# A new order for the first half of a hand-ordered kernel: w_in split ahead of w_out, one triangular mask scaled on ScalarE

## The chip, the cores and the metric

The kernel runs on one core of a Trainium2 chip. The metric is the device time of one execution in microseconds (us). Engines are named as the profile names them: PE (TensorE, matrix multiply), PEld (its weight loads), DVE (VectorE), ACT (ScalarE), POOL (GpSimd), SP (SyncE, which here only issues DMAs).

## What is computed

Three layers follow each other. The first is a linear attention with a per-channel decay, for 2 batches, 8 heads, 768 positions and 48 channels a head:

```python
for t in range(S):
    kt, vt, rt = (k[:, :, t], v[:, :, t], r[:, :, t])
    cur = np.einsum('bhd,bhe->bhde', u[None] * kt, vt)
    y[:, :, t] = np.einsum('bhd,bhde->bhe', rt, state + cur)
    state = w[None, :, :, None] * state + np.einsum('bhd,bhe->bhde', kt, vt)
```

The second, on rows of 384, is a gated convolution: `h = max(x @ w_in, 0)` (384 to 1024), a convolution of three taps along the sequence, a sigmoid of it as the gate, and `(h * gate) @ w_out` (1024 to 384). The third is a mixture of 8 experts (384 to 1024 to 384) in which every row goes to one expert; a row may keep the expert of the row before it.

## The kernel before

Attention is done in 12 chunks of 128 positions (`i` = 0 to 11, six a batch), the gated convolution in 3 groups of about 256 positions a batch and 4 pairs of 128 hidden columns (24 gates `G_b_g_fp`), its second product in 12 tiles of 128 rows, and the experts after that, on rows that are scattered to slots in DRAM and gathered back.

Each piece of work is a Python generator, and each `yield` ends a step. The string `SEQ` (lines 51 to 105) is a list of tokens; one token runs one generator by one step (`advance`, L1161). PE, ACT, DVE and SP execute what the steps emit strictly in that order, each on its own queue, so the order of the tokens is the order of every queue; POOL keeps program order too (`pool_order`, L1167). There is no planner: an instruction whose operand is late holds up everything behind it on its engine.

The tokens that matter here:

- `C` (constants, L253): step 12 makes the identities `id16` (DVE) and `idk` (ACT). Step 13 makes two masks from the triangle `tri0`, both on DVE: `tri32` (L289), which masks the scores of chunks 1 to 5, and `tri` (L290), for chunks 6 to 11. Chunk 0 uses `tri0` itself.
- `L_i` (L188): three loads k, r, v of chunk i. `A_i` (`decay`, L331): POOL scales r and k, PE transposes them (`ptf`), ACT (or DVE) copies them out as `rT`, `kT`; POOL multiplies the two to `kr`.
- `Y_i` (`scores`, L458): PE `psa` (scores), two masked copies `am` on DVE, PE `psy`, for chunks with a state PE adds `psy` from `z`, DVE `yt`, PE transposes (`pxf`), ACT writes the high half of `x1T`, DVE the low half (L511). `Z_i`: the state (PE `psu`, DVE `z`, ACT copies of z). `B_i`: PE `psd`, DVE `dv`.
- `WI_q` (`load_w_in`, L537): a quarter of `w_in`. SP loads it, DVE narrows it from 64 to 32 bits in three instructions (`narrow`, L177, on `f`), ACT scales it and makes the high half (L528, L529), POOL the low half `wi_l` (L156). Quarter q holds the columns of pair fp = q.
- `WO_q` (`load_w_out`, L580): a quarter of `w_out`, two row tiles; each is narrowed on DVE into PSUM (on `ps`), ACT makes the high half, DVE the low half; later PE transposes it and multiplies it with the gate weights.
- `G_b_g_fp` (`gate`, L620): PE `psh` (9 matmuls that read `x1T` and `wi_h`, `wi_l`), ACT `hp`, the three taps (on PE, or ACT and DVE), ACT tanh, DVE `cv`, ACT `g_h`, POOL `g_l`. `H_k` (L241): two matmuls on zeros that nobody reads.
- `O`, `OL`, `OR` (L678): the second product; `R`, `Q`, `S` (route, chances, scatter); `RC`, `SI`: constants of the routing and the clearing of the slots; `W1`, `W2`: expert weights, each loaded by SP, split by ACT (L533) and DVE (L158).

All loads of `w_in`, `w_out`, `W1` and `W2` take turns in three staging buffers (tag `stage`, `bufs=3`): the fourth load waits until the first one's tile has been narrowed or split, and the SP queue waits with it.

Of the kernel before, what the change touches and what calls it, by code (L numbers as in the profile page):

```python
# [55 lines left out]
A_4 CV G_0_0_0 G_0_0_1 A_4 WO_1 Z_3 WO_0 WO_1 Y_3 G_0_0_1 Z_3 L_5 WO_0 L_6 WO_2 Y_3 L_5 G_0_0_1 L_7 Y_2 Z_2 WO_1 A_4 Y_2 A_5 G_0_0_1 A_4 WO_0 WI_2 Y_2  # L56
G_0_0_1 A_4 WO_0 Y_3 Y_2 WO_0 L_6 G_0_0_1 A_5 WO_0 G_0_0_1 Y_4 WO_2 Y_3 A_5 WO_0 B_3 A_5 WI_2 Y_3 WI_2 Z_4 A_5 WO_1 B_3 Z_3 WO_2 L_6 WO_1 Y_4 L_6 WO_2
G_0_0_0 WO_1 G_0_0_2 Z_4 L_7 A_6 T WO_1 A_5 G_0_0_1 WO_1 G_0_0_0 G_0_0_2 A_6 WO_2 B_6 A_5 G_0_0_0 WO_2 B_4 A_6 G_0_0_1 G_0_0_2 Y_3 B_4 WO_2 G_0_0_0
G_0_0_2 Y_3 Y_4 G_0_0_0 Y_3 W1_5_0 A_6 G_0_0_2 Y_5 Y_3 Y_4 G_0_0_0 B_6 Z_4 G_0_0_2 Y_5 G_0_0_2 A_6 WO_1 G_0_0_2 G_0_1_1 A_6 B_6 WO_1 SI G_0_0_2 WO_2
G_0_1_1 G_0_0_2 WO_1 Y_4 A_6 B_5 WO_1 A_6 Y_4 Z_6 L_7 WO_2 A_6 G_0_0_0 WO_1 RC B_5 Y_5 G_0_0_2 G_0_1_2 G_0_1_1 L_7 A_7 G_0_0_0 G_0_1_1 G_0_1_2 G_0_1_1  # L60
G_0_1_2 Y_4 G_0_0_2 Z_6 G_0_1_2 B_7 G_0_1_1 G_0_1_1 WO_3 G_0_1_2 G_0_1_0 G_0_1_2 WO_2 Y_5 G_0_1_2 WO_2 Y_4 A_6 L_10 G_0_1_1 Y_5 Y_6 L_8 G_0_1_2 L_8
G_0_1_1 G_0_1_2 L_8 L_8 G_0_1_1 A_7 G_0_1_2 WO_3 G_0_1_0 G_0_1_0 Y_6 WO_2 Y_6 G_0_1_0 G_0_1_1 WO_3 A_7 G_0_1_0 A_7 A_8 Y_5 A_7 G_0_1_1 G_0_0_3 Z_6 A_7
G_0_0_3 WO_2 L_9 WO_3 WO_3 A_7 Y_5 WO_2 G_0_1_0 G_0_1_0 G_0_1_0 A_7 L_10 B_6 A_8 WO_3 L_9 G_0_1_3 G_0_1_0 WO_2 A_8 Y_6 WO_3 Y_5 G_0_0_3 B_7 WO_2 WO_2
Z_6 A_7 Z_7 G_0_1_3 A_8 L_9 G_0_0_3 G_0_0_3 G_0_1_3 G_0_1_3 G_0_1_3 G_0_0_3 G_0_1_2 G_0_0_3 G_0_1_2 G_0_1_0 O_0_0 Y_5 A_8 G_0_1_3 G_0_0_3 Y_4 G_0_1_3
O_0_0 A_7 G_0_1_3 WO_3 A_8 B_7 G_0_0_3 WO_3 Y_7 G_0_0_3 Y_7 O_0_0 WO_3 G_0_2_0 A_8 B_8 A_8 G_0_1_3 Y_6 L_9 WO_3 WO_3 G_0_1_3 WO_3 WO_3 L_11 B_8 Z_7
A_9 G_0_2_1 B_7 Y_6 Y_7 G_0_0_3 WO_3 G_0_0_3 Y_7 G_0_2_0 WO_3 G_0_1_3 A_9 Z_8 G_0_2_0 G_0_2_1 WO_3 A_8 Z_8 B_8 G_0_1_3 Y_8 Z_7 G_0_2_0 G_0_2_0 Y_6
G_0_2_0 A_9 L_10 G_0_2_1 G_0_2_0 G_0_2_0 Y_6 Y_7 G_0_2_1 G_0_2_1 G_0_2_1 B_9 O_0_1 A_9 Y_7 G_0_2_1 G_0_2_0 Z_7 G_0_2_0 L_10 G_0_2_0 G_0_2_2 A_9 A_9
G_0_2_2 Y_7 G_0_2_1 G_0_2_0 Y_8 O_0_2 A_9 O_0_2 O_0_1 B_9 Y_8 RC G_0_2_1 G_0_2_1 G_0_2_1 Z_8 O_0_2 O_0_0 B_8 G_0_2_3 A_10 O_0_2 Z_9 A_9 O_0_2 A_9 Y_7
G_0_2_1 Y_8 O_0_0 Y_9 Y_8 G_0_2_2 O_0_1 O_0_0 Y_9 Y_8 L_11 G_0_2_3 G_0_2_2 L_11 A_10 G_0_2_2 Y_7 Y_8 O_0_1 O_0_0 O_0_3 G_0_2_2 A_10 A_10 L_11 Y_8
O_0_1 G_0_2_2 G_0_2_2 O_0_1 Y_8 Z_8 G_0_2_3 O_0_1 Y_9 A_10 G_0_2_3 A_10 G_0_2_3 O_0_3 O_0_4 G_0_2_2 A_10 G_0_2_2 O_0_2 A_10 G_0_2_3 O_0_4 G_0_2_3  # L70
G_1_0_3 G_1_0_3 O_0_2 G_0_2_3 Y_9 A_10 G_1_0_3 A_11 Y_10 G_0_2_2 G_0_2_2 A_11 G_1_0_3 Y_9 A_11 B_9 G_1_0_3 G_0_2_3 G_1_0_3 B_10 G_1_0_3 G_0_2_3 W1_6_0
A_11 O_0_3 G_1_0_3 G_0_2_3 G_1_0_3 G_1_0_1 G_0_2_3 O_0_4 G_1_0_3 A_11 O_0_3 Y_10 G_1_0_1 G_1_0_1 G_1_0_1 G_1_0_1 G_1_0_1 A_11 O_0_4 G_1_0_1 Y_10
G_1_0_1 B_9 G_1_0_3 G_1_0_1 O_0_5 O_0_5 Y_9 O_0_4 O_0_4 G_1_0_1 A_11 O_0_5 O_0_3 G_1_0_3 B_10 O_0_4 O_0_5 B_10 G_1_0_0 G_1_0_2 Y_9 G_1_0_2 O_0_5 WO_0
Z_9 A_11 A_11 R_0_0_6 Z_9 O_0_3 Y_11 Y_9 Z_10 WO_1 O_0_3 Y_10 O_0_5 O_0_5 G_1_0_2 Z_10 B_11 G_1_0_0 G_1_0_1 Z_9 R_0_0_6 B_11 Y_11 Y_10 Z_10 R_0_0_6
B_10 R_0_0_6 Y_9 G_1_0_0 Y_10 G_1_0_0 Y_10 G_1_0_2 G_1_0_0 G_1_0_1 G_1_0_2 G_1_0_2 Z_10 B_11 Y_11 G_1_0_0 R_0_0_6 G_1_0_2 G_1_0_0 G_1_0_2 Y_10 R_0_0_6
R_0_0_6 Y_10 R_0_0_6 G_1_0_2 Y_11 G_1_0_0 R_0_0_6 B_11 G_1_0_0 Y_11 G_1_0_0 Y_11 Y_11 Y_11 Y_11 G_1_1_1 G_1_1_1 X G_1_1_1 G_1_0_2 G_1_1_1 R_0_0_6
G_1_1_1 G_1_0_2 G_1_1_2 OR_1_1 OL_1_0 G_1_1_1 G_1_0_2 OL_1_1 G_1_1_1 OL_1_1 G_1_1_2 W1_6_0 R_0_0_6 OL_1_1 G_1_1_1 R_0_0_6 OL_1_0 OL_1_1 OL_1_0 R_0_0_6
OL_1_1 W1_3_0 G_1_1_2 G_1_1_3 OL_1_0 G_1_1_1 G_1_1_2 OL_1_0 G_1_1_1 W1_5_0 R_1_0_2 G_1_1_3 G_1_1_2 SI G_1_1_3 Q_0_0_6 G_1_1_3 G_1_1_3 R_0_0_6 OR_1_1
G_1_1_1 R_0_0_6 G_1_1_3 G_1_1_3 G_1_1_2 OR_1_1 G_1_1_0 G_1_1_2 G_1_1_1 G_1_1_3 G_1_1_2 R_1_0_2 Q_0_0_6 G_1_1_3 G_1_1_3 W1_6_0 G_1_1_2 G_1_1_2 G_1_1_0
G_1_1_3 Q_1_0_2 W1_3_0 G_1_1_2 G_1_2_1 G_1_2_1 OR_1_1 G_1_1_3 Q_0_0_6 G_1_2_1 OR_1_1 G_1_1_0 S_5 G_1_2_1 G_1_1_0 G_1_1_0 G_1_2_1 G_1_2_1 G_1_1_0  # L80
G_1_1_0 G_1_2_1 W1_3_0 G_1_1_0 OR_1_0 OR_1_0 W1_0_0 R_1_0_2 G_1_1_2 G_1_2_3 OR_1_1 W1_0_0 G_1_2_1 S_4 OR_1_0 G_1_1_0 W1_5_0 G_1_2_3 G_1_2_3 G_1_2_3
G_1_2_3 OR_1_0 G_1_2_3 G_1_1_0 G_1_2_1 W1_7_0 Q_1_0_2 OL_1_2 S_2 S_1 R_1_0_2 G_1_2_1 OL_1_2 G_1_2_0 G_1_2_3 W1_7_0 OL_1_2 OL_1_2 OL_1_3 G_1_2_3 OL_1_2
OL_1_3 OL_1_3 G_1_2_0 G_1_2_3 G_1_2_1 OL_1_3 W1_7_0 G_1_2_0 OL_1_3 G_1_2_3 OR_1_0 R_1_0_2 R_1_0_2 G_1_2_0 G_1_2_1 G_1_2_0 G_1_2_3 G_1_2_2 G_1_2_2
R_1_0_2 IO R_1_2_2 G_1_2_2 R_1_0_2 W1_0_0 R_1_2_2 G_1_2_0 G_1_2_3 W1_1_0 S_0 G_1_2_0 R_1_0_2 G_1_2_2 OR_1_2 R_1_2_2 W1_4_0 S_3 Q_1_0_2 G_1_2_2 G_1_2_2
R_1_2_2 OR_1_2 W1_2_0 S_7 R_1_2_2 OR_1_0 Q_1_2_2 OL_1_0 G_1_2_0 G_1_2_2 G_1_2_0 OR_1_2 OR_1_3 WO_3 R_1_2_2 Q_1_2_2 G_1_2_0 OR_1_2 G_1_2_2 R_1_2_2 S_6
G_1_2_2 OR_1_3 FE R_1_2_2 Q_1_2_2 OR_1_2 G_1_2_2 OR_1_3 G_1_2_2 OR_1_3 OR_1_3 OR_1_2 W1_4_0 OL_1_5 R_1_2_2 OL_1_4 OL_1_4 S_8 OL_1_5 FE W1_2_0 OR_1_3
G_1_2_2 OL_1_4 OL_1_4 S_8 OL_1_4 OL_1_5 OL_1_5 OR_1_4 OR_1_4 OL_1_5 OL_1_1 R_1_4_2 W1_4_0 R_1_4_2 FE OR_1_5 S_9 VE R_1_4_2 R_1_4_2 W1_2_0 I_1 OR_1_4
R_1_4_2 ER OR_1_5 OR_1_4 I_3 I_0 ER W2_2_0 R_1_4_2 OR_1_5 R_1_4_2 R_1_4_2 Q_1_4_2 R_1_4_2 OR_1_5 W1_1_0 OH OH F OR_1_4 OR_1_4 Q_1_4_2 OR_1_5 EX EX
Q_1_4_2 OR_1_5 EX I_1 I_0 F EX W2_6_0 EX EX EX I_2 I_3 S_11 VE EX W1_1_0 EX S_10 EX EX EX F M W2_2_0 I_2 U_0_5 U_0_0 W2_2_0 U_0_1 EJ V I_10 V I_12
OL_1_2 U_0_1 U_0_0 S_7 S_6 W2_3_0 U_0_1 U_0_3 W2_6_0 U_0_2 U_0_3 W2_1_0 I_11 U_0_0 U_0_1 U_0_2 W2_3_0 I_10 U_0_4 U_0_3 U_0_4 U_0_0 U_0_2 I_6 U_0_2  # L90
U_0_4 U_0_5 I_11 U_0_1 I_13 S_10 U_0_3 U_0_10 U_0_11 W2_3_0 I_7 U_0_5 I_13 I_6 W2_7_0 U_0_0 U_0_3 I_7 W2_1_0 W2_1_0 I_8 U_0_13 W2_6_0 U_0_6 I_12 U_0_5
U_0_13 U_0_11 I_8 W2_7_0 I_9 U_0_13 OL_1_3 U_0_7 U_0_11 W2_5_0 U_0_13 WO_2 U_0_2 W2_4_0 I_9 W2_7_0 U_0_6 W2_0_0 U_0_11 U_0_10 U_0_10 U_0_12 U_0_10
D_0_5 W2_5_0 U_0_12 U_0_10 U_0_4 U_0_8 W2_5_0 S_11 W1_5_1 S_4 U_0_12 W2_4_0 ME U_0_8 U_0_13 U_0_12 W2_0_0 U_0_9 ME U_0_11 W2_4_0 W2_0_0 W1_6_1 U_0_12
D_0_4 D_0_0 W1_5_1 NX W1_7_1 D_0_13 D_0_5 W1_5_1 U_0_9 D_0_4 U_0_7 D_0_2 D_0_11 W1_6_1 D_0_2 W1_4_1 D_0_12 D_0_0 U_0_7 D_0_13 ME U_0_8 U_0_9 D_0_10
W1_6_1 D_0_3 U_0_7 D_0_11 U_0_8 W1_0_1 W1_4_1 W1_7_1 W1_4_1 D_0_1 U_1_4 W1_0_1 D_0_3 W1_3_1 S_5 W1_7_1 U_0_6 W1_0_1 S_1 U_1_5 W1_3_1 D_0_10 W1_2_1
# [1147 lines left out]
```

## Time and profile before

| | us |
|---|---|
| median of 3 runs (339.04 to 342.38) | 339.89 |
| the profiled execution | 340.96 |
| its span, first to last instruction | 339.2 |

The profile is of one execution. Its first page gives the busy time of each engine over the span and then, in 40 slices, how busy each was. Further views used here: busy times and the clock granted to PE in stretches (windows), the instructions of one engine in order of time (timeline), and the chain of waits that ended last. The start of the span is time zero everywhere below.

### The profile page before, as it was taken

The page shows a single profiled execution, that of the slowest core. Times are in us where ns is not written, and L with a number is a line of the kernel's source. Part 1 is how long each engine was busy: PE and PEld are TensorE (multiplying, and loading weights), DVE is VectorE, ACT ScalarE, POOL GpSimd, SP SyncE. Part 2 cuts the span into 40 slices and gives each one's busy share as a digit, 9 for nine tenths or more (in the row PEclk, how much of TensorE's full clock was granted, in tenths as well). Part 3 has the DMA queues.
Part 4 walks back from the last instruction along what each step waited for, and adds up shares of the span by engine and source line. Part 5 has one row for each costly group of instructions (what it writes and reads, how often), then busy time and mean ns, then how long its engine had stood idle before and what let it go on. Part 6 is the DMA issues. An engine that isn't in the chain of part 4 may idle for free.

```text
span 339.2 us, 8616 instructions
## 1 busy us (share of the span) xinstructions
PE 309.6 (91%) x3227; PEld 214.2 (63%) x3227; DVE 251.9 (74%) x494; ACT 193.0 (57%) x351; POOL 153.6 (45%) x206
## 2 busy tenths in 40 slices
PE   2977999999999999999789886999999998999992
...
GB/s 113 264 231 173 232 161 142 87 211 159 133 65 100 173 64 25 26 225 115 122 230 164 77 263 231 353 146 268 283 281 243 218 273 233 280 68 125 103 75 70
DMA packets 100707, 57.71 MB, mean 170 GB/s; under 512 B 80841, under 2 KB 90376, under 8 KB 100660
## 3 DMA queue, kind: packets, MB, share of 16 engines
...
q8 instruction: 29, 0.48, 0.6%
q14 instruction: 18, 0.15, 0.1%
...
## 4 chain that ended last, share of the span: by engine, by line
PE 44%; issue 33%; DVE 10%; POOL 5%; DMA 3%; ACT 2%; POOLq 1%; SPq 0%; ACTq 0%; DVEq 0%
PE psh L639 13%; PE psx L686 11%; PE pst L653 3%; PE psy L486 3%; PE psa L476 3%; POOL out_dram L905 3%; PE ps L653 2%; DMA slots<-xr,posi 2%; PE psy L498 2%; DVE w1l L158 1%; POOL yb L1017 1%; DMA raw<-in_r_dram 1%; PE psu L430 1%; DVE f L182 1%; PE ptf L361 1%
## 5 line engine op out<-in xcount | busy, mean ns | idle before, releaser
L905 POOL DMA_INDIRECT out_dram<-yb x14 | 13.8, 989 | 100.1 <-DVE yb L1143 95.1
L1134 PE MATMUL py<-w2h,hT 128*64 (+2 forms) x320 | 56.4, 327 | 1.0 <-issue 0.6
L639 PE MATMUL psh<-x1T,wi_h 128*128 128x258 f16 (+2 forms) x288 | 50.4, 276 | 0.0
L1134 PEld LDWEIGHTS <-hT 128*64 128x64 f16 (+1 forms) x480 | 35.3, 105 | 22.5 <-issue 4.0
L1112 PE MATMUL ph<-w1h,xsT 128*128 (+1 forms) x144 | 45.1, 379 | 3.2 <-DVE hr L1094 1.7
L158 DVE SCALAR_TENSOR_TENSOR w1l<-ws,w1h 128x1536 f16<-128x1536 f32 x16 | 30.9, 1950 | 12.3 <-ACT w1h L533 12.3
L639 PE MATMUL psh<-x1T,wi_l 128*128 128x258 f16 (+2 forms) x144 | 39.8, 276 | 0.0
L1134 PE MATMUL py<-w2l,hT 128*64 128x384 f16 (+2 forms) x160 | 37.2, 326 | 0.7 <-issue 0.7
L1112 PEld LDWEIGHTS <-xsT 128*128 128x128 f16 (+1 forms) x216 | 21.4, 102 | 26.1 <-DMA xsT<-yb 2.4
L686 PE MATMUL psx<-wo_h,g_h 128*128 128x384 f16 (+2 forms) x144 | 36.0, 275 | 1.9 <-DVE seq L792 1.5
L686 PE MATMUL psx<-wo_h,g_l 128*128 128x384 f16 (+2 forms) x144 | 35.7, 275 | 1.1 <-POOL g_l L156 1.1
L686 PE MATMUL psx<-wo_l,g_h 128*128 128x384 f16 (+2 forms) x144 | 36.0, 274 | 0.0
L156 POOL TENSOR_TENSOR g_l<-cv,g_h 128x512 f16<-128x512 f32 (+2 forms) x31 | 28.2, 919 | 16.3 <-ACT g_h L167 15.4
L158 DVE SCALAR_TENSOR_TENSOR w2l<-ws,w2h 128x1536 f16<-128x1536 f32 x16 | 27.8, 1753 | 8.3 <-ACT w2h L533 8.3
L639 PEld LDWEIGHTS <-wi_h 128*128 128x128 f16 x288 | 27.4, 99 | 6.0 <-issue 0.2
L686 PEld LDWEIGHTS <-g_h 128*128 128x128 f16 x288 | 22.4, 98 | 13.1 <-DVE seq L792 1.6
L1094 DVE SCALAR_TENSOR_TENSOR hr<-ph,hr 128x512 f16<-128x512 f32 x28 | 18.8, 687 | 15.6 <-ACT hr L1092 13.7
L644 ACT ACTIVATE hp<-psh 128x258 f32<-128x258 f32 (+2 forms) x47 | 18.0, 383 | 20.3 <-PE psh L639 19.7
L1125 ACT COPY hT<-pt 128x1024 f16<-128x1024 f16 x16 | 15.9, 1030 | 21.9 <-PE pt L1123 21.9
L533 ACT ACTIVATE w1h<-ws 128x1536 f16<-128x1536 f32 x16 | 23.5, 1480 | 7.4 <-DMA ws<-in_moe_w_dram 7.4
L1112 PE MATMUL ph<-w1l,xsT 128*128 (+1 forms) x72 | 27.3, 379 | 0.2 <-DVE w1l L158 0.2
L533 ACT ACTIVATE w2h<-ws 128x1536 f16<-128x1536 f32 x16 | 23.8, 1494 | 6.1 <-DMA ws<-in_moe_w_dram 6.1
...
## 6 DMA issues: line engine op xcount, KB each, us to landing
...
```

The source lines that it names most:

```text
L156: eng.tensor_tensor(out=lo, in0=src, in1=hi, op=ALU.subtract)
L158: nc.vector.scalar_tensor_tensor(out=lo, in0=src, scalar=scale, in1=hi, op0=ALU.mult, op1=ALU.subtract)
L533: nc.scalar.activation(out=hi, in_=src, func=AF.Copy, scale=scale)
L639: nc.tensor.matmul(ps[:, 0:n], lhsT=x[:, kk, ft * P:(ft + 1) * P], rhs=x1T[b][:, y, t0:t0 + n], start=(i == 0), stop=(i == 3 * NK - 1))
L644: nc.scalar.activation(out=hp[:, a, o:o + n], in_=ps[:, 0:n], func=AF.Relu, scale=2.0 ** -8)
L653: nc.tensor.matmul(psc[:, a, 0:nd], lhsT=dgs[fp][:, j, a], rhs=hp[:, a, j:j + nd], start=(j == 0), stop=(j == 2))
L686: nc.tensor.matmul(ps[:, c0:c1], lhsT=x[part][:, ft, o:o + P], rhs=y[:, ft, c0:c1], start=(n == 0), stop=(n == 3 * NF - 1))
L905: q = nc.gpsimd.indirect_dma_start(out=dst, out_offset=bass.IndirectOffsetOnAxis(ap=idx.bitcast(U32), axis=0), in_=src, in_offset=None, bo ...
L1094: nc.vector.scalar_tensor_tensor(out=lo, in0=ps, scalar=0.0, in1=hi, op0=ALU.max, op1=ALU.subtract)
L1112: nc.tensor.matmul(ps[hs], lhsT=xs_, rhs=part(W[("w1h", "w1l")[y]], o + kk * HF, HF), start=(n == 0), stop=(n == 3 * NK - 1))
L1125: nc.scalar.copy(out=W["hT"][i], in_=pt)
L1134: nc.tensor.matmul(ps[hs], lhsT=hT[:, x * KF + ft, hs], rhs=part(W[("w2h", "w2l")[y]], o + ft * DM, DM), start=(n == 0), stop=(n == 3 * KF ...
```

## The change

Two things change. In `constants`, `tri32` is made by ACT instead of DVE, and a `yield` behind it makes `tri` a step of its own (a fourteenth `C` token), which the new list places much later. And the first 803 tokens of `SEQ` stand in a new order; the other 477, from `G_1_2_1`'s tenth step on, are the same.

```diff
         nc.scalar.copy(out=idk, in_=id32)
         yield
-        nc.vector.tensor_scalar(out=tri32, in0=tri0, scalar1=-0.5, scalar2=None, op0=ALU.mult)
+        nc.scalar.mul(out=tri32, in_=tri0, mul=-0.5)
+        yield
         nc.vector.tensor_scalar(out=tri, in0=tri0, scalar1=cA, scalar2=-2.0 ** -10, op0=ALU.mult, op1=ALU.mult)
```

```diff
-C LD LD CV C UC C C C LD C LD LD C C WI_0 C L_2 LD C C T T L_2 WO_0 WI_3 T T CV L_2 LD L_2 A_0 A_0 T A_0 A_0 UC T T C T A_0 C Z_0 A_0 Y_0 A_1 Z_0 Y_0
-B_0 CV A_1 A_1 Y_0 CV A_1 A_1 WI_0 WO_1 Y_0 A_2 CV A_1 A_1 B_0 H_2 Y_1 Z_1 Y_1 H_3 A_2 WI_0 B_1 A_2 Z_0 Z_1 Y_0 Y_1 WO_0 H_4 Y_0 WO_0 Y_1 Y_0 B_1 WI_0
-A_2 WO_0 WI_3 WI_1 H_0 L_3 L_3 A_2 Y_1 H_1 A_2 WI_3 WO_0 Y_1 CV WO_1 L_4 GT Y_1 Y_1 WI_3 WO_0 L_3 L_5 A_2 Z_1 L_3 Z_2 CV A_3 Y_1 Y_2 WO_0 H_5 WI_1
-WO_0 H_7 H_6 L_4 B_2 WO_1 WO_1 Y_2 Y_2 L_4 A_3 WI_1 A_3 A_3 L_4 Y_0 WO_0 A_4 WI_2 GT L_5 Y_2 WI_1 Z_2 B_2 A_3 A_3 A_4 GT G_0_0_0 A_3 G_0_0_1 WO_0 Y_2
...
+C LD LD CV C UC C C C LD C LD LD C C WI_0 C L_2 LD C C T T L_2 WI_3 T T CV L_2 LD WI_1 L_3 L_3 L_2 A_0 A_0 T A_0 A_0 UC T T C T A_0 C Z_0 A_0 Y_0 A_1
+Z_0 Y_0 B_0 CV A_1 A_1 Y_0 A_1 A_1 A_2 A_1 WI_0 A_1 B_0 Y_1 Z_1 Y_1 CV Z_1 WI_0 H_0 Y_0 Y_0 Z_0 WO_0 A_2 Y_1 H_6 B_1 A_2 H_4 B_1 A_2 Y_0 H_2 Y_1 Y_0
+GT L_4 CV A_2 L_3 Y_0 WI_0 A_2 A_2 WI_3 Z_2 Y_1 WO_1 L_5 CV Y_2 WI_3 Y_1 Y_1 Y_2 B_2 H_7 WO_0 Y_1 WO_0 Y_1 L_4 B_2 Y_2 L_3 GT CV G_0_0_0 WI_3 H_5 L_4
+A_3 Y_2 Z_1 WO_0 A_3 H_1 WO_0 CV G_0_0_0 H_3 WO_0 WI_1 GT A_3 WI_2 T WO_2 A_3 L_4 WO_0 WO_0 C L_6 A_3 A_4 WO_0 A_3 WO_1 Y_2 WI_1 WI_1 A_3 A_4 A_4 WO_0
+WO_0 WO_0 L_6 WO_1 L_5 Z_2 Z_2 Y_3 WO_0 WO_1 G_0_0_1 WO_1 G_0_0_1 Z_3 Y_2 A_4 G_0_0_1 L_5 Y_3 WO_1 G_0_0_1 WO_1 L_5 WO_0 A_4 G_0_0_1 A_5 Y_2 WO_0 WO_0
...
```

On SP the loads go from `w_in` 0, `w_out` 0, `w_in` 3, ..., `w_out` 1, `w_in` 1 to `w_in` 0, `w_in` 3, ..., `w_in` 1, k and r of chunk 3, `w_out` 0, .... Further on, the differences are smaller shifts. Those named later: `SI`'s DMA (the slots are cleared) comes just ahead of the x1T transpose of chunk 10 instead of behind that of chunk 11; the four groups of 6 matmuls of `OR_1_1` start 33 tokens later; and the scatter `S_5` stands behind the third W1 split of this stretch, not ahead of it, with `S_1` just ahead of it.

## Rows read from the trace of the kernel before

**Rows 1.** The page: the span, and busy us and instructions of each engine.

```profile
span 339.2 us, 8616 instructions
PE 309.6 (91%) x3227; PEld 214.2 (63%) x3227; DVE 251.9 (74%) x494; ACT 193.0 (57%) x351; POOL 153.6 (45%) x206
PE   2977999999999999999789886999999998999992
```

**Rows 2.** Windows: stretch, PE, PEld, DVE, ACT, POOL busy, PEclk, DMA share, GB/s.

```profile
24.00:25.00 1.00, 0.00 (x0) 0.00 (x0) 0.96 (x2) 0.00 (x0) 0.00 (x0) 1.00 0.00 0
25.00:30.00 5.00, 2.36 (x25) 1.97 (x27) 4.86 (x10) 4.00 (x9) 2.81 (x2) 0.61 0.72 207
...
165.00:170.00 5.00, 3.15 (x53) 2.47 (x51) 4.90 (x5) 1.88 (x5) 4.50 (x4) 0.95 0.60 173
170.00:175.00 5.00, 4.13 (x30) 2.83 (x27) 3.98 (x11) 2.68 (x5) 2.01 (x6) 0.50 0.74 259
```

**Rows 3.** Timeline of DVE: start us, us, engine, line, operation, tiles, shapes, count.

```profile
10.07 1.31 DVE L289 TENSOR_SCALAR tri<-tri 128x128 f32<-128x128 f32 x1
12.78 1.29 DVE L480 TENSOR_TENSOR am<-psa,tri 128x512 f32<-128x512 f32 x2 [0.18 <-PE psa L476]
15.65 1.64 DVE L182 SCALAR_TENSOR_TENSOR f<-raw,f 128x768 int32<-128x768 int32 x1
...
60.15 0.68 DVE L668 SCALAR_TENSOR_TENSOR cv<-pst,hp 128x510 f32<-128x510 f32 x1
```

**Rows 4.** Timelines of ACT and POOL, the same columns, early stretch.

```profile
8.79 0.29 ACT L287 CAST idk<-id 128x128 f16<-128x128 f32 x1
14.10 0.59 ACT L167 COPY rT<-ptf 128x512 f32<-128x512 f32 x1 [3.41 <-PE ptf L361]
33.51 0.83 ACT L529 CAST wi_h<-f 128x768 f16<-128x768 f32 x1
...
10.02 1.27 POOL L152 TENSOR_TENSOR kr<-kT,rT 128x512 f32<-128x512 f32 x1
35.28 1.64 POOL L156 TENSOR_TENSOR wi_l<-f,wi_h 128x768 f16<-128x768 f32 x1
```

**Rows 5.** Timeline of PE, the same columns, early stretch.

```profile
13.41 1.09 PE L361 MATMUL ptf<-id,full 128*128 128x128 f32 x8
...
27.64 0.87 PE L506 MATMUL pxf<-id,yt 128*128 128x128 f32 x3 [3.75 <-DVE yt L501]
...
37.73 0.38 PE L639 MATMUL psh<-x1T,wi_h 128*128 128x256 f16 x2
```

**Rows 6.** Chain of waits that ended last: start us, us, what (pieces of one kind merged).

```profile
17.76 0.60 DVE am L480
...
21.18 0.57 DVE ps L182
...
24.35 0.96 DVE f L182
...
29.15 0.47 DVE x1T L156
...
37.90 1.97 PE psh L639 x18
...
42.33 1.49 PE pst L653 x6
...
47.95 1.09 PE psa L476 x16
49.04 1.07 PE psy L486 x32
50.53 0.71 PE psy L498 x16
51.60 0.59 PE ptf L361 x4
```

**Rows 7.** Timelines of DVE and POOL, 159 to 173 us.

```profile
159.45 3.37 DVE L158 SCALAR_TENSOR_TENSOR w1l<-ws,w1h 128x1536 f16<-128x1536 f32 x1
...
171.09 1.75 DVE L158 SCALAR_TENSOR_TENSOR w1l<-ws,w1h 128x1536 f16<-128x1536 f32 x1
...
160.06 1.13 POOL L156 TENSOR_TENSOR g_l<-cv,g_h 128x512 f16<-128x512 f32 x1
```

More of the change, by code (lines that the diff above doesn't have):

```diff
@@ L56 @@
[L56 to L95, printed above, removed]
```

53 lines of the change are left out of this document (46 added, 7 removed).

## The prediction, made before the changed kernel was run

> **What bounds the kernel now.** I read the page first, then the windows, then the timelines of the first 60 us, then the chain of waits. The page says PE: 91% busy, and full in nearly all slices after the fourth [rows 1]. So a change to the first half can win only PE time that is lost: at the start, and around 160 to 215 us, where the digits fall to 6 to 9. The windows show why PE is lost early: from 25 to 30 us it is busy 2.36 of 5 us while DVE is busy 4.86, and the granted clock is 0.61, a mix of its two levels, 2.4 and 1.2 GHz; the clock fell after PE had stood idle [rows 2]. The PE timeline has that hole: 3.75 us ahead of the transposes of chunk 1's y at 27.64, and its releaser is DVE's `yt` [rows 5]. That `yt` was queued behind narrowing of `w_in` 3 and `w_out` 0, which no PE work of that time needed. So before about 38 us DVE sets the pace, and after it PE. From 165 to 170 PE is busy 3.15 of 5 us beside a DVE at 4.90, and the next 5 us run at clock 0.50 [rows 2]: there DVE sets the pace again.
>
> **The change, part by part.** The sum is made by walking the new queues with durations of the old ones. Terms: a `w_in` quarter narrowed is three instructions, 0.56 + 0.97 + 0.96 = 2.49 us, a `w_out` tile 0.48 + 0.57 + 0.57 = 1.62, an `am` 0.60, and each of `dv`, `yt`, `x1T` and a low half of `w_out` 0.47 (one row of each kind stands) [rows 6]. A `z` is two steps, 0.7 together. On PE: `psa` 1.09, `psy` 1.07, its part from `z` 0.71, `ptf` 0.59, one `psh` 0.98 (half of 1.97), taps 1.49 [rows 6]; the short ones (`psu`, `psd`, `pxf`, a pair on zeros) I take at 0.5 and the two of `w_out` at 0.3, estimates below the `ptf` row.
>
> *The masks.* `tri32` costs DVE 1.31 us at 10.07, and `tri` follows. ACT pays about 0.29, as for the cast of the same tile [rows 4], between TR and chunk 1's copy, where it was idle 3.41 us. DVE gains nothing there: the next thing that matters, chunk 0's `am` at 12.78, waited for PE's `psa` [rows 3], and that is not moved. Cover gone, the most it could give is 1.31. Now `tri` at its new place: about 35 us. Bounds: 0.2 by the size of the tile, and 1.64 if it has to stand behind POOL's `wi_l` of that time [rows 4]; I take 0.2.
>
> The trace shows why a small tile took 1.31: POOL was inside `kr` from 10.02 for 1.27 us [rows 3, 4], and the mask ended with it. The Trainium skill, page "SBUF — State Buffer", section "Who interferes with whom", says that DVE in its two-port modes, or with two SBUF inputs while GpSimd reads SBUF, shares a port pair with GpSimd under an exclusive lock, and that the second to issue blocks until the first is done. The trace agrees with 1.31 beside 1.27. By that rule the late `tri` may cost 1.64, and the sum below would be 1.5 instead of 3.0.
>
> *The order, first gate.* Chunk 1's k transposes end at 14.5 on PE [rows 5] and its two ACT copies (0.59 each from 14.10) at 15.3 [rows 4]; the `dg` work that stood between them has moved away. PE then runs `psa1`, `psu1`, zeros, `psy0` (to 18.5), `ptf`, zeros, `psd1`, zeros, `pxf0`: 15.3 + 1.09 + 1.07 + 0.59 + six at 0.5 = 21.05. DVE meanwhile: `am` to 14.07, `w_in` 0 to 17.2 (its third instruction took 1.64 [rows 3]), `dv`, `am`, `z`, `yt`, `am`, `dv` to 20.5; it waits for ACT's half of x1T until 21.5, then `x1T` 22.0, `w_in` 3 to 24.5, `yt1` 25.0. PE reaches the end of `psa2` at 25.55, so `am2` ends at 26.15, one `w_out` tile at 27.8, and x1T of chunk 1 at 28.3. The first gate matmul starts there and not at 37.73 [rows 5]. `w_out` 0 is asked for when `w_in` 0 has been narrowed, at 17.2, as `w_out` 1 was before, behind k and r of chunk 3 (8 heads x 128 x 48 x 4 bytes each, 384 KB in all); the DMA queues stood at 0 GB/s at 24 us [rows 2], so 384 KB more fit before 26.15.
>
> *Second gate.* It needs `w_in` 1: `dv`, `am`, a low half, a `w_out` tile, the quarter: 28.3 + 0.47 + 0.60 + 0.47 + 1.62 + 2.49 = 33.95; ACT two at 0.83, POOL 1.64 [rows 4]: 37.25. Before, the second `psh` began at 37.73 + 0.98 = 38.7. So nine microseconds shrink to 1.4. But PE has by then also done `psy` from z, `psa3`, and two pieces of `w_out`, 0.71 + 1.09 + 0.6 = 2.4, that lay behind it before. Lead 3.8.
>
> *Third station.* The taps behind it need `hp` on ACT, which stands behind a `w_out` half and the z copies, and these behind DVE: 33.95 + 0.18 + 0.6 + 0.47 + 0.2 (`tri`) + 1.62 + 0.7 = 37.7, two z copies 0.7, `hp` 0.4: 38.8. From there PE has taps, `psh`, `ptf`, `pxf`, 0.3, taps, `psd`, `psy3`, `psu`, z part, `psa4` and one `ptf` to do: 9.8, so 48.6. Before, the same set is done at 51.60, where the next `ptf` starts [rows 6]. **Lead 3.0 us.** It is real PE time: the hole of 3.75 and the half clock behind it have gone, and three waits of about 1 us (14.5, 27, 36) have come.
>
> Does DVE follow? From 37.7 to the `cv` of `G_0_0_0` it has 18.2 us of work, so it could be there at 56, where it was at 60.15 [rows 3]. It is not in the way. The rest of the new order (tokens 300 to 803) moves small pieces; I cost it at nothing, because PE is full there. Cover gone, one place is to be named: `SI`'s DMA now stands on SP ahead of the x1T transpose of chunk 10. It needs nothing, so it is issued right behind chunk 9's, several us sooner, on idle queues; it would cost its own length if it were late.
>
> Sum: the profiled execution took 340.96, its span 339.2; minus 3.0 is 337.96, 336.2 of span. The median of the runs was 1.07 lower, so the forecast is 339.89 - 3.0 = 336.9. With the lead between 1.5 (`tri` blocked) and 3.8 (second station) that is 336.1 to 338.4.
>
> **Rivals.**
>
> *R1, the stall at 165 goes too.* PE lost 1.85 us from 165 to 170, 0.87 in the next 5 us, and at clock 0.50 about half of the 4.13 it was busy, 2.07 [rows 2]: 4.8 in all. For it: `OR_1_1`'s groups of 6 matmuls now start later and fill PE there, and a scatter moves off the second W1 split. Against: the DVE order there is nearly the same. Time 339.89 - 3.0 - 4.8 = 332.1; half of it 334.5.
>
> *R2, the lead is swallowed.* From 145 to 210 DVE is nearly full, so PE could arrive 3.0 us sooner and wait 3.0 us longer: 339.9, or 338.6 with the 1.31 that DVE was spared. For it: DVE at 4.90 of 5 [rows 2]. Against: DVE had its own holes before 145, which close when PE feeds it sooner. About 339.3.
>
> *R3, slower: DVE stands behind POOL at more places.* Two of the five W1 splits from 154 to 176 took about 3.35 us (one row stands) and the others 1.75; in the long ones POOL was at work [rows 7]. The Trainium skill's lock (same page and section) names this pair too: `w1l` has two SBUF inputs and `g_l` reads SBUF. If all five meet POOL, DVE, which sets the pace there, is 3 x 1.62 = 4.9 later: 339.89 - 3.0 + 4.9 = 341.8; with no lead left, 344.8. It decides from two more meetings on (2 x 1.62 is over 3.0). Against: a scatter has moved off one split as well as onto another.
>
> **How the numbers follow.** About 1% (3.4 us) is what a measurement here can tell from no change: below 336.5 is faster, above 343.3 slower. Forecast 0.40, of which 0.17 below 336.5; R1 0.25, all below; R2 0.20, all within; R3 0.15, of which 0.11 above 343.3 and 0.04 within. So faster 0.42, same 0.23 + 0.20 + 0.04 = 0.47, slower 0.11. The range reaches over R2 and half of R3 to 342.0 and over most of R1 to 331.5, and leaves out about 0.2. The forecast alone is 336.1 to 338.4.
>
> **What would show it.** Right: no hole of over 2 us on PE between 21 and 30 us, and no half clock there; the first `psh` near 28, the second near 37; the `ptf` behind chunk 4's `psa` near 48.6; a span near 336. R1: PE busy over 4.5 of 5 us around 165 and clock 1.00 behind it. R2: leads at 50 and at 145 us, none at 210. R3: three or more `w1l` over 3 us. I am wrong if the second `psh` comes after 39: then `w_out` 0 landed late, or DVE's sum to `w_in` 1 is short. A `tri` over 1 us would show the blocked mask.

## The result

| | before | changed |
|---|---|---|
| median (lowest to highest), 4 runs each | 339.57 (339.04 to 342.38) | 334.75 (332.83 to 335.70) |
| the profiled execution, its span | 340.96, 339.2 | 335.70, 333.9 |

The ratio is 0.987, with a 95% interval of 0.982 to 0.991: faster by 1.3%. Here and below a median is of all runs of a kernel, a ratio and its interval are of its fast runs alone (those within 1.5% of its fastest), so the two can differ. 336.9 had been forecast, 336.1 to 338.4 if the likeliest case alone held. The time lies in the wide range (331.5 to 342.0), 2.2 under the forecast, on rival R1's half value (334.5), and below the 336.5 under which the prediction calls a time faster (chance 0.42).

The page of the changed kernel, answering [rows 1]: the span, the busy time and the tenths of PE in 40 slices. The line numbers of the changed kernel are one higher from L290 on.

```profile
span 333.9 us, 8627 instructions
PE 305.3 (91%) x3227; PEld 210.3 (63%) x3227; DVE 244.2 (73%) x493; ACT 194.3 (58%) x352; POOL 156.5 (47%) x206
PE   2996899999999999999979797999999989999991
```

The early dip is still there, one slice further on, and PE was busy 4.3 us less. The windows of the changed kernel, with the columns of [rows 2]:

```profile
25.00:30.00 5.00, 1.80 (x23) 1.06 (x23) 2.86 (x6) 1.81 (x6) 4.30 (x5) 1.00 1.03 264
30.00:35.00 5.00, 5.00 (x49) 3.62 (x47) 4.83 (x9) 3.43 (x11) 0.21 (x1) 0.66 0.85 200
...
165.00:170.00 5.00, 5.00 (x69) 4.28 (x67) 3.60 (x9) 3.32 (x7) 4.24 (x6) 1.00 0.25 92
170.00:175.00 5.00, 3.32 (x26) 2.44 (x24) 4.72 (x11) 2.11 (x5) 4.46 (x5) 1.00 0.50 160
```

From 25 to 30 us PE is busy for even less than before (1.80 us, 2.36 before), and now DVE is idle beside it (2.86 of 5); the clock of 0.66 comes one window later. So the early hole was moved and not closed. From 165 to 170 PE is full where it was at 3.15, and the half clock behind it (0.50 from 170 to 175) is gone. The stall is not gone whole: from 170 to 175 PE is busy 3.32 of 5 us, for it waits once for DVE's `oc`, a small tile of the routing:

```profile
172.22 0.39 PE L787 MATMUL pso<-id,oc 128*8 128x128 f16 x4 [1.68 <-DVE oc L779]
```

PE's timeline of the changed kernel names the hole, with two later stations:

```profile
26.25 0.28 PE L640 MATMUL psh<-x1T,wi_h 128*128 128x256 f16 x1
29.68 0.27 PE L640 MATMUL psh<-x1T,wi_h 128*128 128x256 f16 x1 [3.14 <-DVE x1T L156]
...
39.19 0.38 PE L640 MATMUL psh<-x1T,wi_h 128*128 128x256 f16 x2
...
50.15 0.66 PE L362 MATMUL ptf<-id,full 128*128 128x128 f32 x4
```

The first gate begins at 26.25 on the high half of `x1T` and then stands 3.14 us for the low half, which is DVE's. DVE's and SP's timelines say why DVE was late:

```profile
27.41 0.56 DVE L180 TENSOR_SCALAR ps<-raw 128x384 int32<-128x384 int32 x1 [2.07 <-DMA raw<-in_moe_w_out_dram]
...
29.07 0.55 DVE L156 TENSOR_TENSOR x1T<-pxf,x1T 128x384 f16<-128x384 f32 x1
```

```profile
15.81 0.97 SPq L193 DMA_DIRECT2D kt<-in_k_dram  x1
16.82 2.08 SPq L193 DMA_DIRECT2D rt<-in_r_dram  x1
19.01 3.50 SPq L583 DMA_DIRECT2D raw<-in_moe_w_out_dram  x1
```

DVE came to the narrowing of `w_out` 0 at 25.3 and waited 2.07 us for its load. SP asked for that load at 19.01, behind k and r of chunk 3, and the issue alone took 3.50 us. `x1T`'s low half stands behind the narrowing in DVE's queue, and the gate behind `x1T`.

Comparing stations of the two traces shows where 5.7 us went (the spans differ by 5.3). Starts in us; the W1 splits are `w1l` on DVE, counted from the one at 154 us before; the last scatter is POOL's last write to the output:

| | y of chunk 2 | y of chunk 11 | split 1 | split 5 | split 8 | last scatter |
|---|---|---|---|---|---|---|
| before | 42.97 | 141.32 | 154.13 | 175.96 | 205.19 | 333.68 |
| changed | 41.91 | 140.09 | 152.13 | 172.08 | 199.28 | 328.00 |
| lead | 1.1 | 1.2 | 2.0 | 3.9 | 5.9 | 5.7 |

The early part gave 1.1, not 3.0; 0.8 comes between chunk 11's y and the first split, 3.9 from the first to the eighth split. That last part had been costed at nothing. These are differences of one pair of executions; the runs below show how far they vary. (The expectations below were written with the third y named chunk 3's; it is chunk 2's.)

### The profile page after: what moved, and what is told of

It is laid out like the page before. It is cut to its first block, busy times and chain, and to the rows that moved or that the text cites. A ratio compares the mean times of both kernels' runs of the same rounds, so it can differ in the third digit from the quotient of the medians.

```text
span 333.9 us, 8627 instructions
## 1 busy us (share of the span) xinstructions
PE 305.3 (91%) x3227; PEld 210.3 (63%) x3227; DVE 244.2 (73%) x493; ACT 194.3 (58%) x352; POOL 156.5 (47%) x206
## 4 chain that ended last, share of the span: by engine, by line
PE 38%; issue 33%; DVE 9%; POOL 5%; POOLq 1%; DMA 1%; ACT 0%; DVEq 0%
PE psh L640 13%; PE psx L687 11%; PE pst L654 3%; POOL out_dram L906 3%; PE psy L487 2%; PE psa L477 2%; DVE w1l L158 2%; PE psy L499 2%; POOL yb L1018 1%; PE psu L431 1%; PE ps L654 1%; DMA out_dram<-yb 1%; DVE cv L669 1%; DVE xr L158 1%; PE pwt L596 1%
## 5 line engine op out<-in xcount | busy, mean ns | idle before, releaser
L158 DVE SCALAR_TENSOR_TENSOR w1l<-ws,w1h 128x1536 f16<-128x1536 f32 x16 | 27.8, 1750 | 11.6 <-ACT w1h L534 11.6
L156 POOL TENSOR_TENSOR g_l<-cv,g_h 128x512 f16<-128x512 f32 (+2 forms) x31 | 31.0, 1007 | 9.5 <-ACT g_h L167 9.2
```

Of the source, the lines that this page charges most:

```text
L156: eng.tensor_tensor(out=lo, in0=src, in1=hi, op=ALU.subtract)
L158: nc.vector.scalar_tensor_tensor(out=lo, in0=src, scalar=scale, in1=hi, op0=ALU.mult, op1=ALU.subtract)
```

## Experiments

Two theories stood at the start. The first: the gain is early (masks, first gates), as in the forecast's sum. The second: it is made in the W1 splits near 160 us. Twelve kernels were run in three groups, each with runs of the kernel before beside it (median 340.39, 340.76 and 341.12 in these).

### The masks alone

```diff
-        nc.vector.tensor_scalar(out=tri32, in0=tri0, scalar1=-0.5, scalar2=None, op0=ALU.mult)
+        nc.scalar.mul(out=tri32, in_=tri0, mul=-0.5)
+        yield
...
-T A_0 C Z_0
+T A_0 C C Z_0
```

> The order of before, with tri32 made by ScalarE and tri left where it was. Theory A (the mask lay beside a wait for the first scores and gains nothing): 339.6, within 0.7 of the kernel before. Rival B (DVE time near the start is time of the kernel): the mask's 1.31 us come off, 338.3.

Median 341.58 (336.23 to 344.21) against 340.39, while the ratio came out as 0.993 (0.988 to 0.998): the two point opposite ways, and no gain can be read from them. The trace has none: the first split at 154.03 (154.13 before), splits of 3.37 and 3.32 us, the last scatter at 333.57 (333.68). So on the path of this trace the masks are worth nothing, as costed; the times do not settle it.

### The first 300 tokens, and all the others

The first kernel takes the first 300 tokens of the new order and then the old one; the second takes the old order first. Both have the masks of the change. At the joints:

```diff
 G_0_0_2 B_7 G_0_1_2 G_0_1_1 A_6
+SI Z_6 Y_5 G_0_0_0 G_0_1_1
```

```diff
 G_0_1_1 L_7 A_7 G_0_0_0 G_0_1_1 G_0_1_2
+L_8 L_8 A_7 B_7 L_10 G_0_1_1
```

> The first 300 steps in the order of after, all others in the order of before. Theory A (the gain has two places: about 1.0 us of lead at 50 us, and about 4 us between 155 and 185 us that come of the order there): about 1.0 to 1.5 faster than before, 338.3, and two W1 splits over 3 us as before. Rival B (the whole gain is the early lead, and the stretch at 155 us only shows it): 334.5 to 335.5.

> The first 300 steps in the order of before (masks as after), all others in the order of after. Theory A: the splits take 1.75 us each, the clock stays at 1.00 from 165 to 180, 3 to 4 us faster, about 336. Rival B (the early lead is the whole gain): 339.6. Rival C (the later order only pays with the early lead): 338 to 339.

Early tokens alone: median 340.88, ratio 1.000 (0.996 to 1.003). Late tokens alone: 338.53, ratio 0.994 (0.990 to 0.998), although the joint itself cost that kernel a stall at 70 to 80 us (PE busy 6.5 of 10) and chunk 11's y came 4.4 us late. Its splits took 1.75 us and its clock stayed at 1.00 from 165 to 180, as its theory A had said. From the first to the eighth split it needed 45.54 us, the early kernel 49.58 and the kernel before 51.06. So the late part gains, and the early part as it stands gains nothing, where theory A of the early kernel had expected 1.0 to 1.5. In the early kernel chunk 3's y came 4.3 us early (52.21 against 56.47), and I first took this for a lead that was lost later. But chunk 2's y was at 42.75, a lead of 0.2, and chunk 11's at 141.17, a lead of 0.15: the y's between merely stand elsewhere in the order. DVE waited 1.73 us for `w_out` 0 in that kernel too.

### The scatters behind the splits

R1 in the forecast had argued with a scatter that moves off the second split. This kernel is the one before, with only that moved:

```diff
-G_1_1_3 Q_0_0_6 G_1_2_1 OR_1_1 G_1_1_0 S_5 G_1_2_1
+G_1_1_3 Q_0_0_6 G_1_2_1 OR_1_1 G_1_1_0 G_1_2_1
...
-G_1_1_0 G_1_1_0 G_1_2_1 W1_3_0 G_1_1_0
+G_1_1_0 G_1_1_0 G_1_2_1 W1_3_0 S_5 G_1_1_0
```

`S_4` was moved behind `W1_5_0` in the same way.

> The kernel before, with two tokens moved: the scatter S_5 from ahead of the second W1 split of the stretch (expert 3) to just behind it, and S_4 from ahead of the third (expert 5) to just behind it. Theory A (a split that is issued while POOL is in a scatter waits for it and for the g_l behind it): both splits fall from 3.35 to 1.75 us, the clock drop at 170 goes with the stall, 3 us faster, 336.5. Rival D (the splits are long for another reason, or DVE does not set the pace there): splits stay at 3.3 us or the time stays at 339.6.

Median 341.53, ratio 1.003 (1.000 to 1.007); the splits took 3.37 and 3.32 us as before. POOL issues a scatter when its data are there, wherever the token stands between those of other engines. The reason that R1 gave does not hold.

### Which tokens hold the late gain

The change again, as the measure, and its first 748 tokens with the old order for the other 55 (the work from about 152 us on), and the reverse, the kernel before with only these 55 in the new order (and the masks of the change):

```diff
-G_1_1_3 G_1_1_3 W1_6_0 G_1_1_0 G_1_1_2 W1_3_0 G_1_1_2 G_1_2_1 W1_0_0
+OR_1_1 G_1_1_3 W1_6_0 G_1_1_2 G_1_1_2 G_1_1_0 G_1_1_3 Q_1_0_2 W1_3_0
```

> The changed kernel unchanged, as the measure for the three beside it. Expected 334.7 (333 to 336), ratio to the kernel before 0.985 to 0.991; the five W1 splits of 150 to 178 us all near 1.75 us.

> The changed kernel's first 748 tokens, and for the other 55 the order of the kernel before: the new order up to about 152 us alone. Theory L (the last 55 tokens hold the gain): splits of 3.3 to 3.4 us at about 157 and 162, half clock behind 165, the end later than the changed kernel by 3 to 4: 337.7 to 338.7. Theory F (the later start of OR_1_1, and the rest ahead of 748, hold it): the end within 1 us of the changed kernel, 334 to 336.

> The kernel before, with only the tokens behind the 748th in the new order (and tri as a step of its own, right behind tri32): the work from about 152 to 176 us. Theory Z (these 55 tokens are worth about 3.5 us between the first and the eighth W1 split, 50.3 to 46.8, and nothing of it is given back): the first split where it was (154.0), the splits behind it 1.75 us, no half clock behind 165, the eighth split at 201.5 (205.2 before), the median 336.5 to 337.5, 3 to 4 less than the kernel before. Theory P (the zone's gain is given back in the last third, where weights are loaded, as the median of the kernel with the old zone suggests): split 8 earlier, but the end within 1 us of the kernel before.

| kernel | median | ratio (95%) | y of chunk 2 | split 1 | split 5 | split 8 | last scatter |
|---|---|---|---|---|---|---|---|
| changed, again | 334.56 | 0.978 (0.971 to 0.984) | 43.59 | 153.79 | 172.15 | 200.32 | 329.41 |
| 55 tokens old | 335.09 | 0.982 (0.975 to 0.989) | 41.11 | 151.32 | 173.15 | 200.84 | 327.36 |
| 55 tokens new | 337.14 | 0.986 (0.981 to 0.992) | 43.51 | 154.62 | 174.54 | 201.71 | 330.98 |

With the old 55 tokens the time from split 1 to split 5 is 21.83 us, exactly that of the kernel before; with the new ones it is 19.92 in the kernel before, and 19.95 and 18.36 in the changed one's two executions. The kernel that has only these 55 is 4.0 us faster at the median: they hold the late gain. The change itself, run again, came out at a ratio of 0.978, where 0.987 had been measured and 0.985 to 0.991 was expected, and one of its splits took 2.71 us.

How much the late gain is varies. From the first to the eighth split the six kernels with the old tokens there took 49.5 to 51.1 us, and six executions with the new ones 45.5 to 47.2, so the gain is 3.6 between the means and 2.4 to 5.5 for single pairs, of which the pair above (51.06 and 47.15) is one. The two old ones over 50.8 (the kernel before and the one with the scatters moved) had a mean granted clock of 0.77 from 165 to 180 us; those at 49.5 to 49.6 (masks alone, early tokens alone, 55 old ones) had 0.89. How long PE ran at the half clock thus differs between executions of one order.

The windows of the kernel with the 55 old ones show the stall of [rows 2] again, though `OR_1_1` starts late in it:

```profile
165.00:170.00 5.00, 2.60 (x41) 2.15 (x40) 4.86 (x10) 3.56 (x6) 2.61 (x4) 0.85 0.75 211
170.00:175.00 5.00, 5.00 (x36) 3.73 (x35) 3.90 (x14) 1.76 (x4) 3.16 (x6) 0.81 0.59 187
```

Only the first tokens of `OR_1_1` stand late there, but the kernel with one token moved, below, leaves them all at their old places and has the gain. So R1's other reason, the later `OR_1_1`, falls as well. One thing does not fit: by its splits the kernel with the old 55 should end some 2 to 3 us behind the changed one, and its median is only 0.5 behind (its ratio 0.004, which is 1.5 us). In the profiled execution it won 2.2 us back behind split 8 (126.52 us from there to the last scatter, 128.72 in the changed kernel). Over all twelve kernels and the two of the result that stretch takes between 126.0 and 130.0 us with the same instructions, so medians of six runs with ranges of 4 to 7 us do not settle 2 us. The stations before split 8 do.

### One token

Which of the 55? `W1_3_0`'s third step (split 2) stands ahead of the chances (`Q_0_0_6`) that the first scatter waits for in the new order, behind them in the old. The kernel before with this one token moved, and the changed kernel with it moved back (only the place where it is put in is shown):

```diff
-G_1_2_1 G_1_2_1 OR_1_1 G_1_1_3 Q_0_0_6 G_1_2_1
+G_1_2_1 G_1_2_1 OR_1_1 G_1_1_3 W1_3_0 Q_0_0_6 G_1_2_1
```

```diff
-G_1_1_2 G_1_2_1 G_1_1_0 OR_1_0 OR_1_1 Q_0_0_6 G_1_1_0
+G_1_1_2 G_1_2_1 G_1_1_0 OR_1_0 OR_1_1 Q_0_0_6 W1_3_0 G_1_1_0
```

> The kernel before with one token moved: W1_3_0's third step (the second W1 split of the stretch) ahead of the chances that the first scatter waits for. Theory Z1 (a blocked split is most of the zone's loss, and a split that starts ahead of the scatter is not blocked): second split 1.75 us, fifth split 1.6 us or more earlier than in the kernel before (176.0), the end about 1.6 to 2.5 earlier. Theory Z2 (the block only moves: the split makes the scatter late instead, the third split is still blocked, and PE's hole at 165 stays): the fifth split and the end within 0.7 of the kernel before.

> The changed kernel with one token moved: the second W1 split of the stretch (W1_3_0's third step) stands behind the chances that the first scatter waits for, as it did in the kernel before, not ahead of them. Theory L (who is first, split or POOL, decides; the order of these two made the gain at 155 to 180 us): one or two splits are over 3 us again, the fifth split starts 1.6 to 3.2 us later than in the changed kernel (172.1), and the end is later by as much: 336.3 to 338. Theory F (the gain is PE's, from the OR_1_1 groups that start later, and DVE's order there does not matter): splits may be long, but the end stays within 0.7 of the changed kernel.

The first: median 337.02 against 341.12, ratio 0.988 (0.983 to 0.994), split 5 at 173.94 (2.0 earlier), split 8 at 201.13 (4.1 earlier). One token gives what the 55 give. The second: median 334.75 against 334.56 for the change beside it, ratio 0.985 against 0.978 with intervals that overlap, and 47.41 us from the first to the eighth split against 47.15 and 46.53. Moved back alone, the token does not bring the loss back, as theory L had said it would: no split is over 3 us. The splits and POOL's work beside them tell both. First the kernel before, DVE's third split and POOL around the second and third, which belong to [rows 7]:

```profile
164.71 3.32 DVE L158 SCALAR_TENSOR_TENSOR w1l<-ws,w1h 128x1536 f16<-128x1536 f32 x1
...
158.84 1.19 POOL L905 DMA_INDIRECT slots<-xr,posi  x1 [1.08 <-DVE xr L832]
...
165.28 1.13 POOL L156 TENSOR_TENSOR g_l<-cv,g_h 128x512 f16<-128x512 f32 x1
166.57 2.33 POOL L905 DMA_INDIRECT slots<-xr,posi  x1 [0.16 <-issue]
```

Split 2 started 0.61 us behind the scatter, and split 3 0.49 behind the next one (164.22, 1.02 us). POOL's `g_l` followed each scatter at once, and the splits end 1.63 and 1.62 us behind the ends of these `g_l` (161.19 and 166.41): a split seems to do its whole work behind them. What stands behind the third split in DVE's queue is late by as much, and PE waits for it:

```profile
168.93 0.67 DVE L792 TENSOR_TENSOR_SCAN seq<-ca,pso 8x256 f16<-8x256 f32 x1
169.66 0.19 PE L686 MATMUL psx<-wo_h,g_h 128*128 128x9 f16 x1 [1.49 <-DVE seq L792]
```

That is the longest wait of PE in the stall of [rows 2]. The changed kernel:

```profile
154.94 1.75 DVE L158 SCALAR_TENSOR_TENSOR w1l<-ws,w1h 128x1536 f16<-128x1536 f32 x1
159.27 1.75 DVE L158 SCALAR_TENSOR_TENSOR w1l<-ws,w1h 128x1536 f16<-128x1536 f32 x1
...
172.08 1.75 DVE L158 SCALAR_TENSOR_TENSOR w1l<-ws,w1h 128x1536 f16<-128x1536 f32 x1
```

```profile
159.05 1.19 POOL L906 DMA_INDIRECT slots<-xr,posi  x1 [1.38 <-DVE xr L833]
160.30 1.70 POOL L156 TENSOR_TENSOR g_l<-cv,g_h 128x512 f16<-128x512 f32 x1
...
172.21 2.49 POOL L906 DMA_INDIRECT slots<-xr,posi  x1 [0.17 <-issue]
```

Here the splits take 1.75 us and POOL's instructions are the long ones: the `g_l` at 160.30 ends 0.98 us behind split 3, the scatter at 172.21 0.87 behind split 5. The changed kernel with the token moved back has its split 2 at 159.08, now 0.39 us ahead of the scatter, not behind it:

```profile
159.08 1.75 DVE L158 SCALAR_TENSOR_TENSOR w1l<-ws,w1h 128x1536 f16<-128x1536 f32 x1
...
159.47 2.43 POOL L906 DMA_INDIRECT slots<-xr,posi  x1 [1.76 <-DVE xr L833]
```

And the kernel before with the token moved ahead has split 2 at 156.84 for 2.44 us, 0.30 behind a `g_l` (156.54, 1.12 us), and ends 1.62 behind that; its other splits take 1.75 to 1.77. So what decides is when a split starts beside POOL's work, to some tenths of a us, and not the order of the tokens as such: either DVE pays, 0.7 to 1.6 us a split, or POOL does. DVE sets the pace here (4.90 of 5 [rows 2]) and POOL has slack, so the same meeting costs 1.6 us on one side and little on the other. Two blocked splits are 3.2 us, near the 3.9 of the stretch; the half clock behind the stall goes with them, and I have not separated the two. The wait for `oc` that is left in the changed kernel is such a meeting too: the `oc` at 171.01 took 1.07 us beside a `g_l` that had started at 170.93, and 0.18 in the kernel before.

By the Trainium skill, page "SBUF — State Buffer", section "Who interferes with whom", the first to issue holds the shared port pair for the whole instruction and issue order decides who blocks. Over the first eight splits of all fourteen executions the meetings with a `g_l` alone agree: four splits that started 0.03 to 0.30 us behind one took 2.44 to 2.71, and a `g_l` that started 0.29 us or more behind a split ended 0.97 to 0.99 behind it. (Two started within 0.01 us of a split, and there POOL paid.)

The DMA issues on POOL (scatters, and the gather `yb`) do not all agree. A scatter that began 0.13 to 0.39 us behind a split took 2.43 to 2.50 us instead of about 1.0. But splits that began 0.02 to 0.29 us, or 0.70 us and more, behind a scatter took 1.75 to 1.77; and the gather that began 0.29 us ahead of split 7 was itself the late one each time (2.93 to 2.94 us, where most gathers took about 1.0). Only the long splits of the old order, 0.49 and 0.61 us behind a scatter, were held up, and there the `g_l` behind the scatter passed the split although it started later. Whether the scatter, the `g_l` or the two together held them is not shown.

### The load of `w_out` 0

In the changed kernel SP asks for `w_out` 0 behind `w_in` 1 and behind k and r of chunk 3. Two kernels put it ahead of both, or between them:

```diff
-WI_3 T T CV L_2 LD WI_1 L_3 L_3 L_2
+WI_3 T T CV L_2 LD WO_0 WI_1 L_3 L_3 L_2
...
-Z_1 WI_0 H_0 Y_0 Y_0 Z_0 WO_0 A_2 Y_1
+Z_1 WI_0 H_0 Y_0 Y_0 Z_0 A_2 Y_1
```

```diff
+WI_3 T T CV L_2 LD WI_1 WO_0 L_3 L_3 L_2
```

The third has the first of these in its first 300 tokens, and the old order behind them:

> The changed kernel with one token moved: SP asks for w_out 0 ahead of w_in 1 instead of behind it. Both theories: the 2.07 us that DVE waited for w_out 0 at 25.3 and the 3.14 us hole of PE ahead of 29.7 are gone, second gate near 37.3 instead of 39.2. Theory E (a lead won early is kept): the end is 2 us earlier, 332.7, and the W1 splits start 2 us earlier. Theory N (between 60 and 150 us PE and DVE wait for other things and a lead is lost there, as it was in the kernel that had the early order alone): lead at chunk 11's y under 0.7 and the end within 0.7 of the changed kernel, 334 to 335.4.

> The changed kernel with w_out 0 asked for behind w_in 1, but ahead of k and r of chunk 3 (384 KB), so between the changed kernel and the one that asks for it first. Theory B (what delays the load is the bytes ahead of it in the queues): the 384 KB are worth 1 to 1.5 us, DVE's wait of 1.3 to 3.0 us falls to 0 to 1.5, chunk 3's y at 40 to 41.5, the median 332 to 333.5. Theory S (the load can't be asked for before w_in 0 has been narrowed and its buffer is free): asked for at 17, not 19, so about 2 us sooner, and the wait is gone: 331.5.

> The first 300 tokens of the changed kernel with w_out 0 asked for ahead of w_in 1, and the order of the kernel before behind them. Theory E (the early lead is real when the load lands in time, and nothing between 40 and 330 us takes it back): chunk 3's y at 40 (42.97 before), the first W1 split at 150.9 (154.1 before), splits of 3.4 and 3.3 as before, the median 3 less than that of the kernel before, 337.3. Theory N (it is lost when the old order follows): the first split at 154, the end within 1 us of the kernel before.

| kernel | median | beside it: before | ratio (95%) | y of chunk 2 | split 1 | last scatter |
|---|---|---|---|---|---|---|
| `w_out` 0 first | 331.45 | 340.76 | 0.971 (0.965 to 0.977) | 39.47 | 149.16 | 324.08 |
| `w_out` 0 between | 331.97 | 341.12 | 0.974 (0.970 to 0.979) | 40.02 | 150.23 | 321.78 |
| first, and the old order from token 301 | 336.32 | 341.12 | 0.988 (0.982 to 0.993) | 39.06 | 149.78 | 329.49 |

DVE's wait is gone in all three. The kernel with `w_out` 0 first, DVE and then PE:

```profile
25.65 0.55 DVE L180 TENSOR_SCALAR ps<-raw 128x384 int32<-128x384 int32 x1
...
27.31 0.55 DVE L156 TENSOR_TENSOR x1T<-pxf,x1T 128x384 f16<-128x384 f32 x1
```

```profile
27.91 0.27 PE L640 MATMUL psh<-x1T,wi_h 128*128 128x256 f16 x1 [0.97 <-DVE x1T L156]
...
36.17 0.38 PE L640 MATMUL psh<-x1T,wi_h 128*128 128x256 f16 x2
...
47.20 0.65 PE L362 MATMUL ptf<-id,full 128*128 128x128 f32 x4
```

The hole of 3.14 us has become 0.97, and the clock stays at 1.00 through 25 to 40 us. (With the load between, the hole is 1.18 and the clock 0.79 and 0.87 from 25 to 35 us.) The early leads of 3.5 and 3.9 us at chunk 2's y (first and third kernel) are 5.0 and 4.4 at the first split, and the third ends 4.8 (341.12 to 336.32) earlier with the old order behind it: an early lead is kept. Without the moved load the same early tokens had gained nothing (340.88 against 340.39). Early part and late part add: 4.8 and 4.0 (the 55 tokens alone) against 9.3 for the kernel that has both (340.76 to 331.45). The kernel with `w_out` 0 first is 3.1 us under the change beside it by the medians (331.45 and 334.56) and 2.2 by the ratios (0.971 and 0.978, whose intervals overlap); its last scatter comes 3.9 and 5.3 us before those of the changed kernel's two executions.

The buffer that the load needs is free when `w_in` 0 has been narrowed, in the changed kernel at 15.75. With the load between, SP asked for it at 16.16, and in the changed kernel at 19.01: the 3 us are the issues of k and r, 0.97 and 2.08. The load between is also ahead of the 384 KB of k and r, so this kernel alone does not tell the time of the issues from that of the bytes (its median, 331.97, lies between its two theories). The trace of the changed kernel speaks for the issues: the DMA engines moved 315 to 346 GB/s from 16 to 22 us and only 137 from 22 to 24, where SP's issue of `w_out` 0 had just ended (22.51). And four executions with the same first 748 tokens, all with the load behind k and r, got it at different times. DVE's row in the changed kernel again, with the token moved back, and with the 55 old tokens (the changed kernel's stands above):

```profile
28.53 0.56 DVE L180 TENSOR_SCALAR ps<-raw 128x384 int32<-128x384 int32 x1 [3.01 <-DMA raw<-in_moe_w_out_dram]
```

```profile
28.15 0.56 DVE L180 TENSOR_SCALAR ps<-raw 128x384 int32<-128x384 int32 x1 [2.79 <-DMA raw<-in_moe_w_out_dram]
```

```profile
26.80 0.56 DVE L180 TENSOR_SCALAR ps<-raw 128x384 int32<-128x384 int32 x1 [1.27 <-DMA raw<-in_moe_w_out_dram]
```

The waits of 1.27, 2.07, 2.79 and 3.01 go with a y of chunk 2 at 41.11, 41.91, 43.09 and 43.59, and from there to the first split all four take 110.20 to 110.22 us. So the early lead of this order was 1.9, 1.1, -0.1 and, in an execution that was one of the longer ones (336.51), -0.6 us, set for the most part by this one landing and by the clock behind it (0.81, 0.66, 0.53 and 0.50 from 30 to 35 us). Why the landing varies was not separated.

## Why the prediction was right or wrong

**What bounds the kernel: right.** Early PE time and the stretch near 165 us were what could be won, and both were won from.

**Masks: right.** ACT's `tri32` took 0.30 (0.29 costed). The late `tri` took 0.28, near the 0.2 taken; the blocked case of 1.64 did not come: POOL's `wi_l` of that time came later, at 38.52. That it is the place beside `kr` that costs 1.31, as the prediction read, fits the run with the masks alone, where `tri` stood in that place and took 1.31:

```profile
10.55 0.30 ACT L289 ACTIVATE tri<-tri 128x128 f32<-128x128 f32 x1
36.53 0.28 DVE L291 TENSOR_SCALAR tri<-tri,pw 128x128 f32<-128x128 f32 x1
```

**First gate: the failed step.** "384 KB more fit before 26.15" and "asked for when `w_in` 0 has been narrowed, at 17.2" were wrong: `w_in` 0 was done at 15.75, but the request came at 19.01 and the load landed at 27.4. I counted the bytes ahead of it and not the time of SP's issues (0.97 and 2.08 for k and r, 3.50 for itself), and read 0 GB/s at 24 us from a trace in which those loads had not been asked for. The hole that was to close was 3.14 us. With the load in time the first gate was whole at 27.91, so the rest of this walk (28.3) was right.

**Second gate and third station: the walk was right, its start was late.** Predicted and measured, in the changed kernel and with `w_out` 0 first: first gate whole from 28.3, 29.68, 27.91; second gate 37.25, 39.19, 36.17 (its third matmul then waits for `wi_l`, until 40.22 and 37.27); `ptf` behind chunk 4's `psa` done 48.6, 50.81, 47.85. In the chain of the changed kernel the last of them stands as

```profile
49.13 1.09 PE psa L477 x16
50.22 0.59 PE ptf L362 x4
```

so the lead at the third station was 51.60 - 50.81 = 0.8 instead of 3.0, and 3.75 with the load in time. The sum of queue durations was good to 1 us. The announced sign, a second `psh` after 39, came true.

**The rest of the order, costed at nothing: wrong, the second failed step.** The reason given, that PE is full there, does not hold from 165 us on, where the prediction itself had seen DVE set the pace. It gave 0.8 ahead of the first split and 3.9 up to the eighth. The 0.8 belongs to the new order of tokens 301 to 748 (the kernels with the old order there need 12.8 us from chunk 11's y to split 1, the others 12.04) and was not traced further.

**R1 came true by half, for another reason.** The stall at 165 shrank to one wait of 1.68 us and the half clock went, worth 3.9 of the 4.8 priced. It was neither `OR_1_1` nor the moved scatter token, but when a split starts beside POOL's work. **R3 was the right mechanism with the wrong sign:** I had feared more splits behind POOL; none took over 3 us in the changed kernel (one of 2.71 in its second execution). **R2 was wrong:** an early lead is kept, as the kernel with the load in time and the old order behind it shows.

The time came near the forecast by luck: 2.2 too much early (3.0 forecast, 0.8 measured at the third station) and 4.7 too little late (0.8 and 3.9) partly cancel, 336.9 + 2.2 - 4.7 = 334.4, measured 334.75.
